# Reordering the second expert's output sums, and the loads and first matmuls, in a linear attention + MoE + top-1 MoE kernel

## The chip, the core and the metric

The kernel runs on one core of a Trainium2 chip. The metric is the device time of one execution in microseconds (us), taken as the median of the runs. The kernel works in f32 with exact splits of operands into a high and a low part.

## What is computed

Three blocks stand one behind the other. Cut to what matters:

```
# attention, B=2, H=8, S=576, D=64, 128 features
phi(x) = exp(h - max(h)) / sqrt(m),   h = x @ omega.T - |x|^2/2
kv = phi(k).T @ v;  z = sum(phi(k));  out = phi(q) @ kv / (phi(q) @ z + 1e-6)
# MoE 1: 1152 tokens, 512 -> 2048 -> 512
x = gelu_sigmoid(x @ w_in) @ w_out
# MoE 2, top-1: 8 experts, 512 -> 1024 -> 512, capacity 288
expert = argmax(x @ w_gate);  out[i] = gate_weight[i] * relu(x[i] @ w1[e]) @ w2[e]
```

## The kernel before, in words

Every product is three matmuls, high x high, high x low and low x high, added up in PSUM (`mm3`, L100 to L103). Tokens go in four groups of 288 (`GS`), which are columns of the tiles; d_model is four chunks of 128 partitions (`KD`), and an expert's inner width of 1024 is eight chunks m (`NF2`).

**The start.** `om_raw` (omega, twice side by side), then the rows of k, v, k, q, v are loaded on SyncE's queue (SP), each batch and half of the heads with one or two DMAs for its first 512 tokens and two small ones, the "tails", for its last 64 (`load_rows`, L110). TensorE (PE) transposes omega (L164); VectorE (DVE) scales it and splits it into `om_hi` and `om_lo` (L188 to L192). A software pipeline of steps s then does, for four rows of k or q at a time, transposition (`do_T`, L295), split (ScalarE, ACT, at L298; DVE at L305), projection (`do_P`), row maximum (L321), exp (L334), and for k the sums `kvp` (L352). Tile's scheduler fixes each engine's order when the kernel is built; every engine then works through its own list in order.

**The end.** MoE 1 and the two experts run as slots n: in each, `do_h2` makes one inner chunk (12 matmuls into `h_ps`, of which there are two buffers), ACT and DVE turn it into the high and low part of its relu (L876, L877), and two slots later `do_y2` adds that chunk's share to all four output chunks, which are held in four PSUM banks:

```
for c in range(KD):
    dc = slice(c * 128, c * 128 + 128)
    mm3(zps[key][c][:, :GS], hi[:, m % 4, dc], lo[:, m % 4, dc], hhi, hlo, m == 0, m == NF2 - 1)
```

Expert 1 (the second, `key` 1) follows expert 0 slot by slot. Its weights come as eight pieces `eraw` of 512 KB into four buffers; `split_e` turns each into a high part (ACT, `eh`, L863) and a low one (DVE, `el`, L864), and a buffer is loaded again after that. When an expert's sums are full, `slot_z` copies the four banks to `z` (DVE L894, ACT L892), and `slot_rows` does, for each of three blocks of 96 tokens, four transposes into one bank (L899), a masked copy of 96x512 into `base` (`copy_predicated`, DVE L940), the gate weight on ACT (L941) and a store on SP (L942). For expert 0 this lies among expert 1's slots; for expert 1 it comes behind the last sum. Then every engine reads three counters and branches past a fallback (L1030 to L1033) that these inputs do not enter.

Of the kernel before, what the change touches and what calls it, by code (L numbers as in the profile page):

```python
# [35 lines left out]
def linear_attention__moe__top1_moe_kernel(  # L36
# [73 lines left out]
    def load_rows(src, kind, b, p, parts=1):  # L110
        t = attA.tile([128, NU, D], F32, tag="raw", name="qk_raw", bufs=6)
        heads = src[b, 4 * p:4 * p + 4]
        per = 4 // parts
        for i in range(parts):
            hs_ = slice(i * per, (i + 1) * per)
            nc.sync.dma_start(
                out=t[:, JF * per * i:JF * per * (i + 1)].rearrange("p (h j) d -> p h (j d)", j=JF),
                in_=heads[hs_, 0:SF].rearrange("h (p j) d -> p h (j d)", j=JF),
            )
        for h in range(2):  # L120
            nc.sync.dma_start(
                out=t[64 * h:64 * h + 64, 16:18],
                in_=heads.rearrange("(u h) s d -> h s u d", h=2)[h, SF:S],
            )
        raws[kind, b, p] = t
# [4 lines left out]

    om_raw = attA.tile([128, 2, D], F32, name="om_raw")
    nc.sync.dma_start(out=om_raw, in_=omega.unsqueeze(1).to_broadcast([M, 2, D]))
    load_rows(k, "k", 0, 0, parts=2)
    load_rows(v, "v", 0, 0)
    load_rows(k, "k", 0, 1)
    load_rows(q, "q", 0, 0)
    load_rows(v, "v", 0, 1)


    ones_bf = const.tile([TT, 128], BF16, name="ones_bf")  # L140
    nc.vector.memset(ones_bf, 1.0)
    col_minus_p = attA.tile([128, 128], I32, name="col_minus_p")
    nc.gpsimd.iota(col_minus_p, pattern=[[1, 128]], base=0, channel_multiplier=-1)
    ident = const.tile([128, 128], F32, name="ident")
# [16 lines left out]
    om_lo = attA.tile([128, 2, M], F32R, name="om_lo")  # L161
    om_f = attA.tile([128, M], F32, name="om_f")
    ps = bank("A", "om_ps")
    nc.tensor.transpose(ps[:, 0:128], om_raw.rearrange("m a d -> m (a d)"), ident)  # L164
    def place_v(b, p, after=None):
        t = raws.pop(("v", b, p))
        eng = nc.gpsimd if b or p else nc.vector
# [20 lines left out]
    nc.vector.tensor_scalar(om_f, ps[:, 0:M], -scale, None, ALU.mult)  # L188
    for h in range(2):
        r = slice(64 * h, 64 * h + 64)  # L190
        nc.vector.tensor_copy(om_hi[r, h], om_f[r])
        nc.vector.tensor_tensor(om_lo[r, h], om_f[r], om_hi[r, h].bitcast(F32), ALU.subtract)  # L192
    om_hi2 = om_hi.rearrange("p a m -> p (a m)")
    om_lo2 = om_lo.rearrange("p a m -> p (a m)")
# [416 lines left out]
    def slot(n, f):  # L611
        side.setdefault(round(n * 2) / 2, []).append(f)
# [3 lines left out]
    def parts_tile(three):  # L616

        nth[0] += 1
        if three and nth[0] % 3 == 0:
            t = gp.tile([128, 2, GS], F32R, tag="wt", name="ghl", bufs=3)  # L620
            return t[:, 0], t[:, 1]
        return [gp.tile([128, GS], F32R, tag=tag, name=tag, bufs=2) for tag in ("ghi", "glo")]
# [242 lines left out]

    hs, zps = {}, {}

    def do_h2(key, m, wt, tok):
        ps = bank("A", "h_ps")
        hi, lo = wt[m // 4]  # L870
        fc = slice((m % 4) * 128, (m % 4) * 128 + 128)
        for c in range(KD):
            mm3(ps[:, :GS], hi[:, c, fc], lo[:, c, fc], x_hi[:, c, :, tok], x_lo[:, c, :, tok],
                c == 0, c == KD - 1)
        hhi, hlo = parts_tile(True)
        nc.scalar.activation(hhi, ps[:, :GS], ACTF.Relu)  # L876
        nc.vector.scalar_tensor_tensor(hlo, ps[:, :GS], 0.0, hhi.bitcast(F32), ALU.max, ALU.subtract)  # L877
        hs[key, m] = (hhi, hlo)

    def do_y2(key, m, wt):  # L880
        if m == 0:
            zps[key] = y_banks()
        hhi, hlo = hs.pop((key, m))
        hi, lo = wt[2 + m // 4]
        for c in range(KD):
            dc = slice(c * 128, c * 128 + 128)
            mm3(zps[key][c][:, :GS], hi[:, m % 4, dc], lo[:, m % 4, dc], hhi, hlo, m == 0, m == NF2 - 1)

    def do_z_out(key, z):
        for c in range(KD):  # L890
# [5 lines left out]
    def z_rows(z, j):  # L896
        ps = mbank("zt_ps")
        for c in range(KD):
            nc.tensor.transpose(ps[:TT, c * 128:(c + 1) * 128], z[:, c, j * TT:(j + 1) * TT], ident)  # L899
        return ps[:TT, :DM]  # L900

    st = {}

# [28 lines left out]
    def slot_base(i):  # L932
        nc.gpsimd.memset(st["s", i][1], 0.0)
# [59 lines left out]
    for i in range(8):  # L993
        if i < 4:
            slot(NSL + 4, lambda i=i: load_e(st["e", 1], i, 1))
        slot(NSL + 5 + i // 2, lambda i=i: split_e(st["w1"], i, 1))
        if i < 4:
            slot(NSL + 5 + i // 2, lambda i=i: load_e(st["e", 1], i + 4, 1))
    slot(NSL + 9, count_left)
    slot(NSL + 9, do_weights)  # L1000
    slot(NSL + NF2 + 1, lambda: slot_z(0))
    slot(NSL + NF2 + 1, lambda: slot_base(0))
    slot(NSL + NF2 + 3, lambda: slot_rows(0, 0))
    slot(NSL + NF2 + 3, lambda: slot_rows(0, 1))
    slot(NSL + NF2 + 4, lambda: slot_rows(0, 2))

    for n in range(NSL + 2 * NF2 + 2):
        now[0] = n
        if n < NSL:
            do_h(*seq[n])  # L1010
        elif n < NSL + 2 * NF2:
            i, m = divmod(n - NSL, NF2)
            do_h2(i, m, st[f"w{i}"], tokens(2 * i))
        for f in side.pop(n - 0.5, []):
            f()
        if 2 <= n < NSL + 2:
            do_consume(*seq[n - 2])
        elif n >= NSL + 2:
            i, m = divmod(n - 2 - NSL, NF2)
            do_y2(i, m, st[f"w{i}"])  # L1020
        for f in side.pop(n, []):
            f()

    slot_z(1)
    slot_base(1)
    for j in range(TJ):
        slot_rows(1, j)


    n_left = nc.values_load(st["all"][0:1, 0:1], min_val=0, max_val=NP)  # L1030
# [91 lines left out]
```

## Time and profile before

| what | before |
| --- | --- |
| median of 3 runs | 332.81 us (332.39 to 333.35) |
| the profiled execution's own time | 333.84 us |
| its span | 331.9 us |
| PE busy | 317.0 us, 96% of the span |
| DVE, ACT, POOL busy | 178.2, 169.7, 52.3 us |
| DMA, mean over the span | 106 GB/s |

The span is what the profile's rows cover; the execution's own time is 1.94 us longer. PE's matmuls are pipelined and their ends are modelled, so a busy PE can still be a PE that waits for a clock.

### The profile page before, as it was taken

The numbers are of one execution on the slowest core, as the hardware profiler recorded it, in microseconds if no ns is written. First come the engines' busy times: TensorE is split into PE (matmuls) and PEld (weight loads), VectorE is DVE, ScalarE is ACT, GpSimd is POOL, SyncE is SP. The second block draws the span as 40 slices with busy tenths as digits, with TensorE's granted clock in tenths as the row PEclk, the third lists the DMA queues.
The fourth block names the chain that finished last, engine by engine and source line by source line (L and its number), as shares of the span: only waits on it lengthen the run. The fifth ranks groups of instructions, "written<-read, shape, count | busy, mean of one in ns | idle before, by whom it ended". The sixth has DMA issues, their size and how long they took to land.

```text
span 331.9 us, 6635 instructions
## 1 busy us (share of the span) xinstructions
PE 317.0 (96%) x2569; PEld 304.0 (92%) x2569; DVE 178.2 (54%) x444; ACT 169.7 (51%) x445; POOL 52.3 (16%) x77
## 2 busy tenths in 40 slices
PE   5899999999999999999999999999999999998990
PEld 4899999899999999999999998989999999998990
DVE  5568888788579764464544223036614134467222
ACT  2788988889744554454544442234614233364312
POOL 3120311130000143434545200000000001100000
PEclk9999999999999999999999999999999999999996
DMA  6999632410032644344431000704400000482202
GB/s 159 289 292 308 209 136 63 129 61 5 2 126 67 225 157 126 128 128 126 146 124 51 0 2 0 254 2 128 126 2 0 3 0 2 161 264 82 73 0 81
DMA packets 29078, 35.18 MB, mean 106 GB/s; under 512 B 5360, under 2 KB 23792, under 8 KB 29040
## 3 DMA queue, kind: packets, MB, share of 16 engines
q1 hardware_dynamic: 29040, 34.69, 33.8%
q8 instruction: 22, 0.36, 0.5%
q14 instruction: 16, 0.13, 0.1%
HBM read 32.33 MB, written 2.36 MB: 105 GB/s over the span
## 4 chain that ended last, share of the span: by engine, by line
PE 87%; DMA 5%; ACT 2%; SPq 2%; DVE 1%; issue 1%; ACTq 0%; DVEq 0%
PE h_ps L101 13%; PE h_ps L102 12%; PE h_ps L103 12%; PE y L101 7%; PE y L102 7%; PE y L103 7%; PE kvp L352 4%; PE nps L377 4%; DMA eraw<-in_moe_w_dram 3%; PE pj L101 2%; PE t L366 2%; PE pj L102 2%; PE pj L103 2%; PE tp L295 2%; PE wt_ps L505 2%; DMA qk_raw<-in_q_dram 2%
## 5 line engine op out<-in xcount | busy, mean ns | idle before, releaser
L640 DVE TENSOR_TENSOR glo<-g,ghi 128x288 fp32r<-128x288 f32 x27 | 12.3, 457 | 39.0 <-ACT g L639 39.0
L633 ACT ACTIVATE g<-h_ps 128x288 f32<-128x288 f32 x32 | 13.2, 411 | 30.0 <-PE h_ps L103 25.1
L321 DVE TENSOR_REDUCE nb<-pj 128x4 f32<-128x512 f32 (+1 forms) x40 | 25.0, 630 | 4.8 <-PE pj L103 4.3
L249 DVE TENSOR_SCALAR wf<-wraw 128x512 int32<-128x512 int32 x32 | 13.4, 423 | 24.9 <-POOL win2l L262 10.8
L864 DVE TENSOR_TENSOR el<-eraw,eh 128x1024 fp32r<-128x1024 f32 x16 | 19.5, 1222 | 13.0 <-ACT eh L863 13.0
L101 PE MATMUL pj<-om_hi,xh 128*128 128x256 f32 x72 | 24.3, 338 | 0.7 <-ACT qp L334 0.6
L637 ACT ACTIVATE ghi<-h_ps 128x288 fp32r<-128x288 f32 x27 | 11.1, 411 | 26.8 <-PE h_ps L103 26.8
L863 ACT CAST eh<-eraw 128x1024 fp32r<-128x1024 f32 x16 | 16.7, 1048 | 14.6 <-PE h_ps L102 7.4
L255 DVE SCALAR_TENSOR_TENSOR wf<-wraw,wf 128x512 int32<-128x512 int32 x32 | 22.9, 716 | 0.4
L334 ACT ACTIVATE qp<-pj,nb 128x128 f32<-128x128 f32 x72 | 21.9, 392 | 0.2
L252 DVE SCALAR_TENSOR_TENSOR wf<-wraw,wf 128x512 int32<-128x512 int32 x32 | 21.8, 685 | 0.2
L102 PE MATMUL pj<-om_lo,xh 128*128 128x256 f32 x72 | 21.4, 298 | 0.0
L334 ACT ACTIVATE kp<-pj,nb 128x128 f32<-128x128 f32 x72 | 21.4, 387 | 0.0
L103 PE MATMUL pj<-om_hi,xl 128*128 128x256 f32 x72 | 21.2, 294 | 0.0
L298 ACT CAST xh<-tp 128x256 fp32r<-128x256 f32 (+1 forms) x40 | 14.6, 364 | 11.5 <-PE tp L295 11.2
L101 PE MATMUL h_ps<-x_hi,win0h 128*128 128x288 f32 x64 | 20.0, 313 | 0.0
L352 PE MATMUL kvp<-vt,kp 128*128 128x65 f32 (+1 forms) x144 | 19.8, 270 | 0.0
L101 PE MATMUL h_ps<-x_hi,win3h 128*128 128x288 f32 x64 | 19.7, 307 | 0.0
L101 PE MATMUL h_ps<-x_hi,win2h 128*128 128x288 f32 x64 | 19.6, 306 | 0.0
L101 PE MATMUL h_ps<-x_hi,win1h 128*128 128x288 f32 x64 | 19.4, 303 | 0.0
L305 DVE TENSOR_TENSOR xl<-tp,xh 128x256 fp32r<-128x256 f32 (+1 forms) x40 | 15.6, 390 | 6.8 <-ACT xh L298 6.6
L101 PE MATMUL h_ps<-x_hi,eh 128*128 128x288 f32 x64 | 19.3, 301 | 0.0
(250 smaller groups left out, 1073.8 us busy)
## 6 DMA issues: line engine op xcount, KB each, us to landing
wraw<-in_moe_w_in_dram SPq DMA_DIRECT2D x16, 512.0 KB, 4.4
wraw<-in_moe_w_out_dram SPq DMA_DIRECT2D x16, 512.0 KB, 3.6
eraw<-in_moe_w_dram SPq DMA_DIRECT2D x16, 512.0 KB, 4.7
qk_raw<-in_v_dram SPq DMA_DIRECT2D x4, 512.0 KB, 5.3
qk_raw<-in_q_dram SPq DMA_DIRECT2D x4, 512.0 KB, 5.7
qk_raw<-in_k_dram SPq DMA_DIRECT2D x3, 512.0 KB, 5.7
out_dram<-zer SPq DMA_DIRECT2D x2, 576.0 KB, 5.5
out_dram<-base SPq DMA_DIRECT2D x6, 192.0 KB, 2.8
```

Of the source, the lines that this page charges most:

```text
L101: nc.tensor.matmul(o, lh, rh, start=start, stop=False)
L102: nc.tensor.matmul(o, lh, rl, start=False, stop=False)
L103: nc.tensor.matmul(o, ll, rh, start=False, stop=stop)
L252: nc.vector.scalar_tensor_tensor(f, high, -0x40000000, f, ALU.bitwise_and, ALU.bitwise_or)
L255: nc.vector.scalar_tensor_tensor(f, low, 29, f, ALU.logical_shift_right, ALU.bitwise_or)
L298: nc.scalar.copy(xh[:, :n], tp[:, :n])
L305: nc.vector.tensor_tensor(xl[:, :n], tp[:, :n], xh[:, :n].bitcast(F32), ALU.subtract)
L321: mark["M", s] = nc.vector.tensor_reduce(nb[:, :nj], pj[:, :nj * M].rearrange("p (a m) -> p a m", m=M), AX, ALU.min)
L334: nc.scalar.activation(t[:, i], pj[:, i * M:(i + 1) * M], ACTF.Exp, bias=nb[:, i:i + 1], scale=-1.0)
L352: nc.tensor.matmul(ps[:, o:o + n], kp[:, i], vts[p][:, u, c0:c0 + n], start=(f == 0), stop=(f == NU - 1))
L863: nc.scalar.copy(hi, tv)
L864: nc.vector.tensor_tensor(lo, tv, hi.bitcast(F32), ALU.subtract)
```

## The change

It does five things. (1) The tails of the first k go out from ACT's queue instead of SP's, behind a one-column copy on ACT. (2) Seven small bf16 matmuls into an unused bank stand ahead of omega's transposition on PE, four behind it; their results are not read. (3) One of the two casts to `om_hi` goes from DVE to ACT. (4) Expert 1's chunks m = 1 to 7 are kept in tiles of their own, its `do_h2` run without `do_y2` between them, and the last four pieces of its weights are split one to two slots apart, each behind the last relu. (5) `do_last` makes the output sums with the output chunk c outside: m = 0 to 3, then the chunk before goes out (three transposes, masked copy of 96x3x128, gate weight, one store), then m = 4 to 7. Expert 0's rows are worked on within chunk 0. Only chunk 3 is left behind the last sum, in three pieces of 96 tokens with banks and tiles of their own.

```diff
--- before.py
+++ after.py
@@ -118,7 +118,7 @@
                 in_=heads[hs_, 0:SF].rearrange("h (p j) d -> p h (j d)", j=JF),
             )
         for h in range(2):
-            nc.sync.dma_start(
+            (nc.scalar if parts > 1 else nc.sync).dma_start(
                 out=t[64 * h:64 * h + 64, 16:18],
                 in_=heads.rearrange("(u h) s d -> h s u d", h=2)[h, SF:S],
             )
@@ -130,15 +130,25 @@
 
     om_raw = attA.tile([128, 2, D], F32, name="om_raw")
     nc.sync.dma_start(out=om_raw, in_=omega.unsqueeze(1).to_broadcast([M, 2, D]))
-    load_rows(k, "k", 0, 0, parts=2)
+    ones_bf = const.tile([TT, 128], BF16, name="ones_bf")
+    nc.vector.memset(ones_bf, 1.0)
+    first = attA.tile([TT, 1], F32, name="first")
+    with tc.issue_after(nc.scalar.copy(first, ones_bf[:, 0:1]).ins):
+        load_rows(k, "k", 0, 0, parts=2)
     load_rows(v, "v", 0, 0)
     load_rows(k, "k", 0, 1)
     load_rows(q, "q", 0, 0)
     load_rows(v, "v", 0, 1)
 
 
-    ones_bf = const.tile([TT, 128], BF16, name="ones_bf")
-    nc.vector.memset(ones_bf, 1.0)
+    idle = bank("M", "idle")
+
+    def spin(n):
+        for _ in range(n):
+            nc.tensor.matmul(idle[:, 0:256], ones_bf, ones_bf.unsqueeze(1).to_broadcast([TT, 2, 128]),
+                             start=True, stop=True)
+
+    spin(7)
@@ -161,7 +171,8 @@
     om_lo = attA.tile([128, 2, M], F32R, name="om_lo")
     om_f = attA.tile([128, M], F32, name="om_f")
     ps = bank("A", "om_ps")
-    nc.tensor.transpose(ps[:, 0:128], om_raw.rearrange("m a d -> m (a d)"), ident)
+    with tc.issue_after(nc.tensor.transpose(ps[:, 0:128], om_raw.rearrange("m a d -> m (a d)"), ident).ins):
+        spin(4)
@@ -188,7 +199,7 @@
     nc.vector.tensor_scalar(om_f, ps[:, 0:M], -scale, None, ALU.mult)
     for h in range(2):
         r = slice(64 * h, 64 * h + 64)
-        nc.vector.tensor_copy(om_hi[r, h], om_f[r])
+        (nc.scalar.copy if h else nc.vector.tensor_copy)(om_hi[r, h], om_f[r])
         nc.vector.tensor_tensor(om_lo[r, h], om_f[r], om_hi[r, h].bitcast(F32), ALU.subtract)
     om_hi2 = om_hi.rearrange("p a m -> p (a m)")
@@ -865,6 +876,8 @@
 
     hs, zps = {}, {}
 
+    spare = {}
+
     def do_h2(key, m, wt, tok):
         ps = bank("A", "h_ps")
         hi, lo = wt[m // 4]
@@ -872,9 +885,15 @@
         for c in range(KD):
             mm3(ps[:, :GS], hi[:, c, fc], lo[:, c, fc], x_hi[:, c, :, tok], x_lo[:, c, :, tok],
                 c == 0, c == KD - 1)
-        hhi, hlo = parts_tile(True)
-        nc.scalar.activation(hhi, ps[:, :GS], ACTF.Relu)
-        nc.vector.scalar_tensor_tensor(hlo, ps[:, :GS], 0.0, hhi.bitcast(F32), ALU.max, ALU.subtract)
+        if key == 1 and m:
+            for s in "hl":
+                if s not in spare:
+                    spare[s] = pool_of["in", 2].tile([128, NF2 - 1, GS], F32R, tag=f"win2{s}", name=f"hh{s}")
+            hhi, hlo = spare["h"][:, m - 1], spare["l"][:, m - 1]
+        else:
+            hhi, hlo = parts_tile(True)
+        mark["ra"] = nc.scalar.activation(hhi, ps[:, :GS], ACTF.Relu)
+        mark["rv"] = nc.vector.scalar_tensor_tensor(hlo, ps[:, :GS], 0.0, hhi.bitcast(F32), ALU.max, ALU.subtract)
         hs[key, m] = (hhi, hlo)
 
     def do_y2(key, m, wt):
@@ -886,6 +905,13 @@
             dc = slice(c * 128, c * 128 + 128)
             mm3(zps[key][c][:, :GS], hi[:, m % 4, dc], lo[:, m % 4, dc], hhi, hlo, m == 0, m == NF2 - 1)
 
+    def split_late(i):
+        if i < 4:
+            split_e(st["w1"], i, 1)
+        else:
+            with tc.issue_after(mark["ra"].ins), tc.issue_after(mark["rv"].ins):
+                split_e(st["w1"], i, 1)
+
     def do_z_out(key, z):
         for c in range(KD):
             if c % 2:
@@ -898,6 +924,63 @@
         for c in range(KD):
             nc.tensor.transpose(ps[:TT, c * 128:(c + 1) * 128], z[:, c, j * TT:(j + 1) * TT], ident)
         return ps[:TT, :DM]
+
+    def do_last(wt):
+
+        z, base = scratch(1)
+        nc.gpsimd.memset(base, 0.0)
+        zps[1] = y_banks()
+        mk = st["mk", 1].bitcast(I32)
+        r0 = 2 * GS
+        g0 = 2 * TJ
+        rows = out[r0:r0 + GS, :].rearrange("(j p) d -> p j d", p=TT)
+
+        def sums(c, ms):
+            dc = slice(c * 128, c * 128 + 128)
+            for m in ms:
+                hhi, hlo = hs[1, m]
+                hi, lo = wt[2 + m // 4]
+                mm3(zps[1][c][:, :GS], hi[:, m % 4, dc], lo[:, m % 4, dc], hhi, hlo, m == 0, m == NF2 - 1)
+
+        def chunk(c):
+            dc = slice(c * 128, c * 128 + 128)
+            ps = mbank("zt_ps")
+            for j in range(TJ):
+                nc.tensor.transpose(ps[:TT, j * 128:(j + 1) * 128], z[:, c, j * TT:(j + 1) * TT], ident)
+            nc.vector.copy_predicated(base[:, :, dc], mk.unsqueeze(2).to_broadcast([TT, TJ, 128]),
+                                      ps[:TT, :TJ * 128].rearrange("p (j d) -> p j d", j=TJ))
+            nc.vector.tensor_tensor(base[:, :, dc], base[:, :, dc],
+                                    gw[:, g0:g0 + TJ].unsqueeze(2).to_broadcast([TT, TJ, 128]), ALU.mult)
+            nc.sync.dma_start(out=rows[:, :, dc], in_=base[:, :, dc])
+
+        half = NF2 // 2
+        for c in range(KD):
+            sums(c, range(half))
+            if c:
+                chunk(c - 1)
+            else:
+                slot_rows(0, 0)
+                slot_rows(0, 1)
+            sums(c, range(half, NF2))
+            if c == 0:
+                slot_rows(0, 2)
+            if c < KD - 1:
+                nc.scalar.copy(rows_of(z[:, c]), in_order(zps[1][c][:, :GS]))
+        c = KD - 1
+        dc = slice(c * 128, c * 128 + 128)
+        pss = [mbank("zt_ps"), mbank("zt_ps"), bank("A", "zt_ps")]
+        zl = [z[:, c, 0:TT]] + [pool_of["out", 0].tile([128, 2048], F32, tag=f"wout0{s}", name="zl")[:, 0:TT] for s in "hl"]
+        for j in range(TJ):
+            nc.vector.tensor_copy(rows_of(zl[j]), in_order(zps[1][c][:, :GS])[:, j * TT // JF:(j + 1) * TT // JF])
+        for j, ps in enumerate(pss):
+            nc.tensor.transpose(ps[:TT, 0:128], zl[j], ident)
+            nc.vector.copy_predicated(base[:, j, dc], mk[:, j:j + 1].to_broadcast([TT, 128]), ps[:TT, 0:128])
+            if j < TJ - 1:
+                nc.scalar.activation(base[:, j, dc], base[:, j, dc], ACTF.Copy, scale=gw[:, g0 + j:g0 + j + 1])
+            else:
+                nc.vector.tensor_scalar(base[:, j, dc], base[:, j, dc], gw[:, g0 + j:g0 + j + 1], None, ALU.mult)
+        nc.sync.dma_start(out=rows[:, 0, dc], in_=base[:, 0, dc])
+        nc.sync.dma_start(out=rows[:, 1:, dc], in_=base[:, 1:, dc])
 
     st = {}
 
@@ -993,16 +1076,13 @@
     for i in range(8):
         if i < 4:
             slot(NSL + 4, lambda i=i: load_e(st["e", 1], i, 1))
-        slot(NSL + 5 + i // 2, lambda i=i: split_e(st["w1"], i, 1))
+        slot(NSL + (5, 5, 6, 6, 9, 11, 12, 14)[i], lambda i=i: split_late(i))
         if i < 4:
             slot(NSL + 5 + i // 2, lambda i=i: load_e(st["e", 1], i + 4, 1))
     slot(NSL + 9, count_left)
     slot(NSL + 9, do_weights)
     slot(NSL + NF2 + 1, lambda: slot_z(0))
     slot(NSL + NF2 + 1, lambda: slot_base(0))
-    slot(NSL + NF2 + 3, lambda: slot_rows(0, 0))
-    slot(NSL + NF2 + 3, lambda: slot_rows(0, 1))
-    slot(NSL + NF2 + 4, lambda: slot_rows(0, 2))
 
     for n in range(NSL + 2 * NF2 + 2):
         now[0] = n
@@ -1017,14 +1097,12 @@
             do_consume(*seq[n - 2])
         elif n >= NSL + 2:
             i, m = divmod(n - 2 - NSL, NF2)
-            do_y2(i, m, st[f"w{i}"])
+            if i == 0:
+                do_y2(i, m, st[f"w{i}"])
+            elif m == NF2 - 1:
+                do_last(st[f"w{i}"])
         for f in side.pop(n, []):
             f()
-
-    slot_z(1)
-    slot_base(1)
-    for j in range(TJ):
-        slot_rows(1, j)
 
 
     n_left = nc.values_load(st["all"][0:1, 0:1], min_val=0, max_val=NP)
```

**Where instructions stand now: the start, SP and ACT.** `qk_raw` are the loaded rows, the 64x2x64 ones the tails. SP's list before:

```order
L132 DMA om_raw<-in_omega_dram 128x2x64
L116 DMA qk_raw<-in_k_dram 128x2x256 x2
L121 DMA qk_raw<-in_k_dram 64x2x64 x2
L116 DMA qk_raw<-in_v_dram 128x4x256
L121 DMA qk_raw<-in_v_dram 64x2x64 x2
```

SP's list now:

```order
L132 DMA om_raw<-in_omega_dram 128x2x64
L116 DMA qk_raw<-in_k_dram 128x2x256 x2
L116 DMA qk_raw<-in_v_dram 128x4x256
L121 DMA qk_raw<-in_v_dram 64x2x64 x2
L116 DMA qk_raw<-in_k_dram 128x4x256
```

ACT's list now (before it had the table load and then the casts to `xh`):

```order
L136 ACT_TABLE_LOAD
L136 CAST first<-ones_bf 96x1
L121 DMA qk_raw<-in_k_dram 64x2x64 x2
L202 CAST om_hi<-om_f 64x128
L309 CAST xh<-tp 128x256 x4
```

The order of omega and k on SP is as it was; two issues have left SP's list ahead of v, and stand on ACT ahead of its first cast.

**Expert 1's weights and relus on ACT.** `eh` are pieces of weights, `ghi`, `ghl` and `hhh` relus, `z` expert 0's sums. Before:

```order
L863 CAST eh<-eraw 128x1024
L876 ACTIVATE ghl<-h_ps 128x288
L863 CAST eh<-eraw 128x1024
L892 COPY z<-y_3733 128x288
L892 COPY z<-y_3735 128x288
L863 CAST eh<-eraw 128x1024
L876 ACTIVATE ghi<-h_ps 128x288
L863 CAST eh<-eraw 128x1024
```

Now:

```order
L895 ACTIVATE hhh<-h_ps 128x288
L874 CAST eh<-eraw 128x1024
L918 COPY z<-y_3747 128x288
L918 COPY z<-y_3749 128x288
L895 ACTIVATE hhh<-h_ps 128x288 x2
L874 CAST eh<-eraw 128x1024
L895 ACTIVATE hhh<-h_ps 128x288
L874 CAST eh<-eraw 128x1024
L895 ACTIVATE hhh<-h_ps 128x288 x2
L874 CAST eh<-eraw 128x1024
```

The copies of `z` now stand behind one late piece instead of two, and the last three pieces stand between the relus of a stretch in which PE does nothing but `do_h2`.

**The end on DVE.** Before:

```order
L894 COPY z<-y_4100 128x288
L894 COPY z<-y_4102 128x288
L940 COPY_PREDICATED base<-p_mk,zt_ps 96x512 x3
L1030 TENSOR_LOAD all_ni
```

Now:

```order
L950 COPY_PREDICATED base<-p_mk,zt_ps 96x3x128
L952 TENSOR_TENSOR base<-base,gw 96x3x128
L974 COPY z<-y_4194 128x96
L974 COPY zl<-y_4194 128x96 x2
L977 COPY_PREDICATED base<-p_mk,zt_ps 96x128 x3
L981 TENSOR_SCALAR base<-base,gw 96x128
L1108 TENSOR_LOAD all_ni
```

Behind the last sum DVE has seven short instructions where it had a copy of 128x288 and three masked copies of 96x512.

## Rows read from the trace of the kernel before

**Rows 1.** the page, part 4, whole span: the chain that ended last, by engine

```profile
PE 87%; DMA 5%; ACT 2%; SPq 2%; DVE 1%; issue 1%; ACTq 0%; DVEq 0%
```

**Rows 2.** the chain, 0 to 20 us: start us, us, what it was

```profile
2.29 0.73 SPq L121
...
3.70 0.60 SPq L116
...
7.57 5.96 DMA qk_raw<-in_q_dram
...
13.67 0.30 PE tp L295
```

**Rows 3.** waits of PE, whole span: us in total, times, longest

```profile
PE tp L295 <- DMA qk_raw<-in_q_dram: 1.3, 1, 1.3
...
PE y L101 <- ACT z L892: 0.9, 1, 0.9
...
PE y L101 <- DVE z L894: 0.4, 1, 0.4
```

**Rows 4.** windows: us, busy us of each engine, PEclk, DMA share, GB/s

```profile
2.30:4.20 1.90, 0.44 (x1) 0.18 (x1) 0.97 (x5) 0.00 (x0) 1.59 (x9) 1.00 0.92 254
4.20:5.60 1.40, 1.11 (x4) 0.71 (x4) 0.71 (x3) 0.37 (x1) 0.00 (x0) 1.00 0.69 111
...
9.00:13.50 4.50, 3.38 (x25) 3.04 (x24) 3.44 (x9) 3.04 (x12) 0.00 (x0) 1.00 1.00 296
13.70:40.00 26.30, 26.30 (x238) 26.30 (x238) 18.45 (x48) 22.57 (x79) 5.92 (x10) 1.00 0.95 286
```

**Rows 5.** timeline of PE, 9 to 10.1 us: start us, us, engine line op

```profile
9.00 0.41 PE L103 MATMUL pj<-om_hi,xl 128*128 128x256 f32 x1
...
10.04 0.28 PE L103 MATMUL pj<-om_hi,xl 128*128 128x256 f32 x1
```

**Rows 6.** timeline of ACT, 293 to 303 us: idle before and releaser in brackets

```profile
293.81 1.05 ACT L863 CAST eh<-eraw 128x1024 fp32r<-128x1024 f32 x1 [2.78 <-DMA eraw<-in_moe_w_dram]
...
302.25 1.05 ACT L863 CAST eh<-eraw 128x1024 fp32r<-128x1024 f32 x1 [1.00 <-DMA eraw<-in_moe_w_dram]
```

**Rows 7.** groups of ACT by form: count | busy us, mean ns

```profile
L863 ACT CAST eh<-eraw 128x1024 fp32r<-128x1024 f32 x16 | 16.7, 1048 | 14.6 <-PE h_ps L102 7.4 <-DMA eraw<-in_moe_w_dram 6.3 <-PE y L102 0.8
...
L876 ACT ACTIVATE ghi<-h_ps 128x288 fp32r<-128x288 f32 x10 | 4.1, 410 | 10.5 <-PE h_ps L103 10.4
```

**Rows 8.** groups of DVE by form: count | busy us, mean ns

```profile
L864 DVE TENSOR_TENSOR el<-eraw,eh 128x1024 fp32r<-128x1024 f32 x16 | 19.5, 1222 | 13.0 <-ACT eh L863 13.0
L305 DVE TENSOR_TENSOR xl<-tp,xh 128x256 fp32r<-128x256 f32 x32 | 13.4, 419 | 6.8 <-ACT xh L298 6.6
...
L877 DVE SCALAR_TENSOR_TENSOR glo<-h_ps,ghi 128x288 fp32r<-128x288 f32 x10 | 4.5, 453 | 8.1 <-ACT ghi L876 8.0
...
L305 DVE TENSOR_TENSOR xl<-tp,xh 128x128 fp32r<-128x128 f32 x8 | 2.2, 275 | 0.0
```

**Rows 9.** timeline, 322 us to the end

```profile
322.38 0.30 PE L103 MATMUL y<-ghl,el 128*128 128x288 f32 x1
...
323.60 2.18 DVE L940 COPY_PREDICATED base<-p_mk,zt_ps 96x512 f32<-96x512 int32 x3 [0.82 <-PE zt_ps L899]
324.35 2.18 ACT L941 ACTIVATE base<-base,gw 96x512 f32<-96x512 f32 x3 [1.23 <-DVE base L940]
...
324.37 0.64 PE L899 MATMUL zt_ps<-ident,z 128*96 128x128 f32 x4 [0.66 <-DVE base L940]
325.10 1.77 SPq L942 DMA_DIRECT2D out_dram<-base  x3
```

**Rows 10.** instructions of L1033, 300 us to the end: duration ns, first and last start

```profile
L1033 SPq EVENT_SEMAPHORE  x9: 17/17/17, 329.8 to 330.4; - x9
...
L1033 PEldq COMPARE_BRANCH  x1: 4094/4094/4094, 325.8 to 325.8; - x1
```

**Rows 11.** instructions of L942, 300 us to the end: issue to landing

```profile
DMA to landing us min/median/max: 2.1/2.8/4.1
```

## The prediction

> **What bounds the kernel now.** I read the chain that ended last first. It runs through PE for 87% of the span [rows 1], so time is won only where the chain leaves PE, or where PE has less to do. It leaves PE at the start, for a moment when expert 1 begins its output sums, and at the end.
>
> *Start.* The chain there is SP's queue, one issue behind the other: the two k tails from 2.29 us, v at 3.70, q at 7.57; then q's transfer of 5.96 us; then PE's first transposition of q at 13.67 [rows 2]. PE waited 1.3 us for it [rows 3]. While the tails were issued little came in: 111 GB/s at a DMA share of 0.69 between 4.2 and 5.6 us, against 296 GB/s at 1.00 between 9 and 13.5 [rows 4]. From 13.7 to 40 us PE is busy 26.30 of 26.30 us [rows 4], so what it gains before 13.7 it keeps.
>
> *Middle.* At 299 to 301 us PE waits 0.9 and 0.4 us for expert 0's sums to leave their banks [rows 3], because those copies stand behind weight splits on ACT and DVE. Nothing else holds PE for long after that.
>
> *End.* The last sum ends at 322.68, which I call T (322.38 + 0.30). Behind it stand transposes, three masked copies of 0.73 us, three scalings of 0.73 and three stores; the last store is issued at 325.10 + 1.77 - 0.32 = 326.55, taking an issue as 0.32 us (estimate from a store's start to the group's end) [rows 9]. The span closes at 331.9, T + 9.2.
>
> **The change part by part.** I sum against the profiled execution (333.84 us, span 331.9), which stood 0.3% above the median of 332.81, and apply the difference to the median.
>
> *K tails on ACT.* Two issues leave SP ahead of v: 3.70 - 2.29 = 1.41 us [rows 2]. Everything on SP up to q is issued that much earlier. The tails still move their bytes, now beside v; ACT issues them in a stretch in which it does no work (0.00 us busy from 2.3 to 4.2 us [rows 4]), and the cast of `om_hi` that stands behind them replaces 0.3 us of DVE, so both cost nothing while k's rows are still on their way. The gain is at most 1.41 and, if the 16 DMA engines were the limit and not the issue, nothing. The rows speak for the issue up to 9 us: at 0.69 the engines had room. After 9 us they are full [rows 4], which eats some of it, as do the tails themselves. I take **-1.2**, between 0 and -1.4.
>
> The Trainium skill, "Trainium Kernel Development and Optimization", Key Constraints, says that DMAs issued from several engines run on the same 16 DMA engines and that a second issuer saves only the sequencer's issue time. By that rule the term lies between 0 and the issue time too; where the engines are the limit it is 0, which is the first rival.
>
> *Small matmuls.* PE works at the lower of its two levels until about 9.2 us: the same 256 columns take 0.41 us at 9.00 and 0.28 at 10.04 [rows 5]. The difference of 0.13 is near the 0.11 between 256 columns at 1.2 and at 2.4 GHz; the PEclk column shows 1.00 all the while, so I go by durations. Eleven matmuls of 256 columns are about 11 x 0.21 = 2.3 us at the lower level, in a PE that did one matmul between 2.3 and 4.2 us [rows 4]; they cover nothing up, and cost nothing unless omega's transposition comes behind them. If the level rises earlier, PE reaches q's rows sooner, but q's rows set when it goes on. They are worth at most the 0.1 us by which PE's wait (1.3) is shorter than the 1.41 above, and a margin. **0.0**, between -0.1 and +0.5 (some of the first seven ahead of omega).
>
> *The order of the attention.* With the loads, Tile's order of the attention steps moves slightly: the third step of decoding the first weights comes earlier on DVE and its cast earlier on ACT. In 13.7 to 40 us DVE has 18.45 of 26.30 us busy and ACT 22.57 [rows 4], so both have room: **0.0**, +-0.3. POOL's list does not change.
>
> *Expert 1's sums late.* The wait for the banks goes, 0.9 + 0.4 us [rows 3]: expert 1's sums now begin six `do_h2` later. **-1.3**. What is late next: PE runs `do_h2` alone, 12 matmuls of some 0.13 us, 1.6 us for each chunk, on two buffers. Each chunk needs 0.41 us of ACT and 0.45 of DVE, and a late split takes 1.05 on ACT and 1.22 on DVE [rows 7, 8]: with a split 1.46 and 1.67 us. Over one chunk DVE is 0.07 late, over two with a split each 0.14, and the split that still stands ahead of a relu costs its part of the slack. I take **+0.3**, between 0 and +0.6.
>
> *Chunks leaving one by one.* PE's sums are the same 96 matmuls. Of the 12 transposes behind the last sum, 9 move ahead of it: 9 x 0.12 = **+1.1** on PE before the end, 0.12 being (0.64 - 0.28) / 3, the spacing of four transposes [rows 9]. Masked copies, gate weights and stores of chunks 0 to 2 lie beside 3.2 us of sums each: a masked copy of 384 columns is under the 0.73 of 512 [rows 9], its scaling on DVE no dearer, 1.5 of 3.2 us. Expert 0's rows go the same way, on ACT. SP has five stores instead of three; only the last two count.
>
> *Behind the last sum.* DVE's forms of 256 and 128 columns are 0.42 and 0.28 us [rows 8], so 96 columns come to 0.24 and a small form of 128 to 0.28. Three copies of 96 columns end at T + 0.04 + 0.72 = T + 0.76, three masked copies at T + 1.6, the last scaling at T + 1.9, and the last store is issued at T + 1.95, against T + 3.9 now. ACT's two scalings and the first store lie beside this. So the last issue comes 1.95 us earlier. What follows is less sure. SP's nine semaphore steps run from 329.8 to 330.4, and PE's branch past the fallback takes 4.09 us from 325.8, to 329.9 [rows 10]: two things end together, and stores take 2.1 to 4.1 us to land [rows 11]. Lower bound: PE's branch keeps its length; it follows the last transposition, at about T + 0.8, by three register loads, so it begins near T + 2.3 instead of T + 3.1, and the gain is 0.8. Upper bound: only landing counts, and a half as large store lands in 2.1 instead of the third one's 3.7 (330.3 - 326.55): 1.95 + 1.6 = 3.5. I take **-1.5**, nearer to the branch, whose row is the plainer one.
>
> Sum: -1.2 + 0.0 + 0.0 - 1.3 + 0.3 + 1.1 - 1.5 = **-2.6 us**: 331.2 for the profiled execution, **330.2 us** for the median, 0.8% faster.
>
> **The rivals.**
>
> *DMA engines, not issue, hold q.* For it: share 1.00 from 9 us on, and a transfer that takes 5.96 us after its issue [rows 2, 4]. Against it: the 0.69 before. It takes away 1.2: 331.4 us.
>
> *Landing alone ends the kernel.* For it: the times to land spread to 4.1 with three stores close together [rows 11], and smaller ones leave earlier now. Against it: PE's branch ends no earlier than SP's steps begin. It gives 2.0 more: 328.2 us.
>
> *Little moves.* The first rival together with the lower bound of the end and the upper one of the buffers: -1.3 + 0.6 + 1.1 - 0.8 = -0.4, 332.4 us.
>
> *Late splits hold up expert 1* (slower). If a piece of weights lands after ACT has come to its cast, ACT stands there with the relus behind it, both buffers fill, and PE stops where it had output sums to do before. That happened to ACT already: 2.78 us at 293.81, 1.00 at 302.25 [rows 6]. A split that stands whole between a chunk and its relu costs 1.05 + 0.41 + 0.45 + 1.22 = 3.1 us [rows 7, 8] where two buffers give 1.6; three such lose 4.5: 330.2 - 0.3 + 4.5 = 334.4 us. It decides from the point where a late piece lands after about 305 us; the last one landed at 302.25, 3 us before, and the loads start as early as before.
>
> That the small matmuls do not raise the clock at all would change at most 0.1 us here and is no case of its own.
>
> **How the numbers follow.** The forecast has 0.55, with 329.2 to 331.2 as its own range from the bounds of its terms; DMA-bound start 0.17; landing alone 0.10; little moves 0.12; late splits 0.06. A change of 0.3%, 1.0 us, is about what a measurement can tell from none. The first three are faster by more: 0.82. Little moves is the same: 0.12. Late splits are slower: 0.06. The range 328.3 to 331.9 takes in the forecast, the DMA-bound start and the nearer half of the landing case; left out are late splits, little moves and the far end of landing, some 2 in 10.
>
> **What would show it.** Start: q issued on SP near 6.2 us, PE's first transposition of q near 12.4 instead of 13.67, and 256 columns at 0.28 us well before 9. If q is issued at 6.2 and still lands at 13.5, the first rival is right. Middle: no wait of PE for `z`, and waits of at most 0.6 us in all for buffers of `h_ps` between 297 and 307 us; longer ones behind a cast that waits for a DMA would be the slower rival. End: last sum to the end of the span 7.7 us instead of 9.2; PE's branch still 4 us, if I have weighed it rightly. Waits of PE between 14 and 100 us that are not there now would mean that the reordered attention cost something I put at nothing.

## The result, and the profile after

| what | before | after |
| --- | --- | --- |
| median | 332.43 us (6 runs, 331.94 to 333.35) | 329.74 us (6 runs, 329.09 to 330.20) |
| ratio | | 0.9903, 95% interval 0.9875 to 0.9931 |
| profiled execution, its span | 333.84, 331.9 us | 330.05, 328.0 us |

The ratio is an estimate of its own and not the quotient of the two medians, which is 0.992. The change makes the kernel faster by 2.7 us on the medians. The prediction was 330.2 us, -2.6. The two profiled executions are 3.9 us apart in span, 1.2 more than the medians, since the one of before lay above every other run of its kernel. So a difference between these two traces is not yet one between the kernels.

The page of the changed kernel, parts 1 and 4:

```profile
PE 318.8 (97%) x2580; PEld 305.8 (93%) x2580; DVE 180.8 (55%) x451; ACT 168.7 (51%) x447; POOL 52.7 (16%) x77
...
PE 95%; ACT 1%; DMA 1%; DVE 0%; issue 0%; SPq 0%; ACTq 0%
```

PE has 95% of the chain where it had 87 [rows 1], and DMA 1% where it had 5: q's transfer is no longer a link. Its waits, whole span (us in total, times, longest):

```profile
PE idle L148 <- DVE ones_bf L134: 1.1, 1, 1.1
PE pj L101 <- ACT qp L345: 0.4, 1, 0.4
PE zt_ps L976 <- DVE z L974: 0.4, 1, 0.4
PE tp L306 <- DMA qk_raw<-in_k_dram: 0.3, 1, 0.3
```

The waits for q (1.3) and for expert 0's banks (0.9 and 0.4) [rows 3] are gone, and none for `h_ps` has come.

**Start.** ACT's queue issues the tails while SP issues k. SP's queue (start us, us):

```profile
2.29 0.47 SPq L116 DMA_DIRECT2D qk_raw<-in_v_dram  x1
...
6.15 0.59 SPq L116 DMA_DIRECT2D qk_raw<-in_q_dram  x1
```

q is issued at 6.15 instead of 7.57 [rows 2], and takes 5.0 us to about 11.15. The windows beside [rows 4]:

```profile
4.20:5.60 1.40, 1.20 (x5) 0.80 (x5) 0.59 (x3) 0.46 (x2) 0.00 (x0) 1.00 0.99 274
9.00:13.50 4.50, 4.50 (x35) 4.30 (x34) 3.35 (x9) 3.09 (x12) 0.28 (x1) 1.00 0.87 255
```

The engines that stood at 0.69 and 111 GB/s from 4.2 to 5.6 us now move 274. From 9 to 13.5 us PE is busy throughout, for 3.38 of 4.50 us before. What holds PE now is its own level (timeline of PE):

```profile
10.17 0.38 PE L102 MATMUL pj<-om_lo,xh 128*128 128x256 f32 x1
10.38 0.28 PE L103 MATMUL pj<-om_hi,xl 128*128 128x256 f32 x1
...
12.28 0.27 PE L306 MATMUL tp<-ident,qk_raw 128*128 128x128 f32 x1
```

256 columns take 0.28 us from 10.38 on; before they did from 9.57 on, with eleven matmuls fewer ahead. PE reaches q's rows at 12.28 instead of 13.67, 1.1 us after they landed. ACT's exps stand close behind as the next bound: in `e8_oldsplit` (below), whose lists are the same up to there, the rise comes at 9.4, the first `kvp` then wait for the exps one after the other, and PE comes to q's rows at 12.30 all the same.

**End.** Timeline behind the last sum, which ends at 319.81 + 0.29 = 320.10:

```profile
319.81 0.29 PE L103 MATMUL y<-hhh,el 128*128 128x288 f32 x1
...
320.14 0.26 DVE L974 COPY z<-y 128x96 f32<-128x96 f32 x1 [0.41 <-PE y L103]
320.31 0.41 DVE L974 COPY zl<-y 128x96 f32<-128x96 f32 x2
...
320.81 0.71 DVE L977 COPY_PREDICATED base<-p_mk,zt_ps 96x128 f32<-96x128 int32 x3
...
321.56 0.28 DVE L981 TENSOR_SCALAR base<-base,gw 96x128 f32<-96x128 f32 x1
321.62 0.33 SPq L982 DMA_DIRECT2D out_dram<-base  x1
322.05 0.37 SPq L983 DMA_DIRECT2D out_dram<-base  x1
```

The last store is issued at T + 1.95, as worked out, and the span ends at T + 7.9 (before T + 9.2). The instructions of the fallback's branch, L1111 (duration ns, first and last start us):

```profile
L1111 SPq EVENT_SEMAPHORE  x9: 17/17/17, 325.9 to 326.5; - x9
...
L1111 PEldq COMPARE_BRANCH  x1: 3397/3397/3397, 322.2 to 322.2; - x1
L1111 SPq COMPARE_BRANCH  x1: 45/45/45, 322.5 to 322.5; - x1
...
L1111 DVEq COMPARE_BRANCH  x1: 72/72/72, 323.4 to 323.4; - x1
...
L1111 DVEq EVENT_SEMAPHORE  x1: 21/21/21, 326.6 to 326.6; - x1
```

PE's branch takes 3.4 us (4.1 before, [rows 10]). But SP, too, does nothing between its branch at 322.5 and 325.9, and DVE nothing between 323.4 and 326.6. DVE is the last to come past it; I had read PE's row alone. In the kernel before it was ACT:

```profile
L1033 ACTq COMPARE_BRANCH  x1: 50/50/50, 328.0 to 328.0; - x1
...
L1033 ACTq EVENT_SEMAPHORE  x1: 17/17/17, 330.6 to 330.6; - x1
```

Being last past the branch is not yet being what ends the kernel. SP's closing steps show no wait in the changed kernel:

```profile
L1195 SPq EVENT_SEMAPHORE  x12: 17/28/28, 326.5 to 327.9; - x12
```

### The profile page after: what moved, and what is told of

Its sections match the earlier page's. It is cut to its first block, busy times and chain, and to the rows that moved or that the text cites. A ratio compares the mean times of both kernels' runs of the same rounds, so it can differ in the third digit from the quotient of the medians.

```text
span 328.0 us, 6667 instructions
## 1 busy us (share of the span) xinstructions
PE 318.8 (97%) x2580; PEld 305.8 (93%) x2580; DVE 180.8 (55%) x451; ACT 168.7 (51%) x447; POOL 52.7 (16%) x77
## 4 chain that ended last, share of the span: by engine, by line
PE 95%; ACT 1%; DMA 1%; DVE 0%; issue 0%; SPq 0%; ACTq 0%
PE h_ps L101 14%; PE h_ps L102 13%; PE h_ps L103 13%; PE y L101 8%; PE y L102 8%; PE y L103 8%; PE kvp L363 5%; PE nps L388 4%; PE pj L101 3%; PE tp L306 3%; PE pj L102 3%; PE pj L103 3%; PE t L377 3%; PE wt_ps L516 2%; PE lgt_ps L696 1%; PE wg_ps L526 1%
## 5 line engine op out<-in xcount | busy, mean ns | idle before, releaser
L260 DVE TENSOR_SCALAR wf<-wraw 128x512 int32<-128x512 int32 x32 | 13.4, 423 | 24.7 <-POOL win2l L273 10.7
L266 DVE SCALAR_TENSOR_TENSOR wf<-wraw,wf 128x512 int32<-128x512 int32 x32 | 22.9, 717 | 0.4
L263 DVE SCALAR_TENSOR_TENSOR wf<-wraw,wf 128x512 int32<-128x512 int32 x32 | 22.5, 708 | 0.2
L103 PE MATMUL h_ps<-x_hi,win0l 128*128 128x288 f32 x64 | 19.2, 300 | 0.0
L102 PE MATMUL h_ps<-x_lo,win0h 128*128 128x288 f32 x64 | 19.2, 300 | 0.0
```

Source lines behind the costliest of these rows:

```text
L102: nc.tensor.matmul(o, lh, rl, start=False, stop=False)
L103: nc.tensor.matmul(o, ll, rh, start=False, stop=stop)
L260: nc.vector.tensor_scalar(f, high, 3, 0x3FFFFFF8, ALU.logical_shift_left, ALU.bitwise_and)
L263: nc.vector.scalar_tensor_tensor(f, high, -0x40000000, f, ALU.bitwise_and, ALU.bitwise_or)
L266: nc.vector.scalar_tensor_tensor(f, low, 29, f, ALU.logical_shift_right, ALU.bitwise_or)
```

## The experiments

Theory at the outset: the start gives about half, by q's earlier issue and by something in the attention's order; the end gives the other half; the small matmuls do nothing by the clock. Each kernel was timed in five rounds beside the kernel before, which took 332.4, 332.3 and 331.9 us in the three groups (e1 to e4; e5 to e8; e9 to e12). The changed kernel was timed beside 332.43 us only, in the runs of the result. So where a kernel of the third group is set against its 329.74, the two kernels before are 0.5 us apart, and so much of a difference need not be the kernels'.

### The start alone

`e1_start`: the kernel before with the diff's parts (1) to (3).

> The kernel before with the change's start alone (k tails on ScalarE, the eleven small matmuls, one cast of om_hi on ScalarE); the end is the old one. Theory: the start is worth what the last transposition of the attention showed between the two traces, 1.4 us at q and about 2.0 us by 78 us: 330.4 to 331.0 us where the kernel before takes 332.4, PE's first transposition of q at 12.3 +-0.3 instead of 13.67. Rival: part of the 2.0 us was only that one execution of the kernel before was a slow one (333.84 against a median of 332.4); then the start is worth 0.5 to 1.0: 331.4 to 331.9. Waits of PE for z (0.9 + 0.4 us) are back in both.

330.93 us, ratio 0.996 (0.9945 to 0.9975): -1.4 us, at the upper end of the theory's range. q's first transposition is at 12.21, and the attention's last one is won by 2.05 us against the profiled execution of before (77.65 for 79.70). The medians give 1.4, so part of the 2.05 was that execution, as the rival says; `e2_end`, which has the old start, does its last transposition at 79.11, 1.46 behind this one. PE's waits at the end:

```profile
PE zt_ps L910 <- DVE base L951: 0.7, 1, 0.7
PE y L101 <- DVE z L905: 0.5, 2, 0.4
```

The wait for the banks is 0.5 us in the old end with the new start, not 1.3.

### The end alone

`e2_end`: the changed kernel with the old start.

> The changed kernel with the old start (tails on SP, no small matmuls, both casts on VectorE); the end is the new one. Theory: waits for z -1.3, nine transpositions +1.0, behind the last sum -1.3, nothing for buffers: -1.6, so 330.8 us; q first transposed near 13.7. Rival one: the rest of the end does nothing but pay for the transpositions, 331.8 or more. Rival two: the end carries nearly all of the 2.7 us, 329.9 or less, and the start little. Start and end act on stretches that PE keeps apart, so the two parts should add up to 2.7 +-0.4.

331.00 us, ratio 0.9969 (0.9954 to 0.9984): -1.4 us. With e1 it adds up to -2.8, for -2.7 in the change. PE waits 1.1 us for q again and not at all for banks. Behind the last sum (321.07 + 0.29) stand 7.6 us.

### Without the small matmuls

`e3_nospin`:

```diff
-    spin(7)
-    with tc.issue_after(nc.tensor.transpose(ps[:, 0:128], ...).ins):
-        spin(4)
+    nc.tensor.transpose(ps[:, 0:128], ...)
```

> The changed kernel without the eleven small matmuls. Theory: they do nothing; 256 columns of f32 take 0.41 us until 9 to 10.4 us either way, so 329.7 +-0.4 us, the same as the changed kernel. Rival one: they raise the clock in most executions and the profiled one was an exception: 330.3 to 331.0. Rival two: they put the rise off (10.2 us with them against 9.2 in the kernel before): without them the rise is at 9.2 and the time 329.1 or less.

330.13 us, ratio 0.9939 (0.9921 to 0.9956): 0.4 above the changed kernel, at the edge of the theory's range. The clock is not the reason: here 256 columns take 0.28 us from 8.8 us on, earlier than in the changed kernel. The time is lost later. First `nps` and last `tp` (timeline of PE), in the kernel before:

```profile
26.54 0.72 PE L377 MATMUL nps<-kvs,qt 128*128 128x65 f32 x5
...
79.70 0.27 PE L295 MATMUL tp<-ident,qk_raw 128*128 128x128 f32 x1
```

in the changed kernel:

```profile
25.43 1.06 PE L388 MATMUL nps<-kvs,qt 128*128 128x65 f32 x8
...
77.72 0.27 PE L306 MATMUL tp<-ident,qk_raw 128*128 128x128 f32 x1
```

and without the small matmuls:

```profile
25.08 1.06 PE L379 MATMUL nps<-kvs,qt 128*128 128x65 f32 x8
...
78.31 0.27 PE L297 MATMUL tp<-ident,qk_raw 128*128 128x128 f32 x1
```

53.2, 52.3 and 53.2 us. The lists of PE, ACT and DVE differ between them in this stretch: with the matmuls that nobody reads, Tile's scheduler writes the attention in another order. Why it does was not looked into.

### The tails back on SP

`e4_tails_sp`: `nc.scalar if parts > 1 else nc.sync` is `nc.sync` again.

> The changed kernel with the k tails back on SP; small matmuls and the cast on ScalarE stay. Theory: SP's queue held q, so q is issued 1.4 us later, at 7.6 us, and PE waits for it again: first transposition of q at 13.4 to 13.7, 1.2 to 1.4 us slower: 330.9 to 331.1. Rival: PE at its lower level is the bound up to q now, and landing 1.4 us later than 11.15 us costs only 0.3 us there: 330.0.

331.77 us, ratio 0.9983 (0.9971 to 0.9995): 2.0 above the changed kernel, more than either. PE's waits:

```profile
PE tp L306 <- DMA qk_raw<-in_q_dram: 0.8, 1, 0.8
...
PE t L377 <- ACT wt L518: 0.3, 1, 0.3
...
PE xps L430 <- DVE xr L408: 0.3, 1, 0.3
```

q's first transposition is at 13.00, 0.7 us behind the changed kernel. The rest arises later, in the attention, whose lists differ again on PE, ACT and DVE: first `nps` and last `tp` are here

```profile
25.89 1.06 PE L388 MATMUL nps<-kvs,qt 128*128 128x65 f32 x8
...
79.83 0.27 PE L306 MATMUL tp<-ident,qk_raw 128*128 128x128 f32 x1
```

53.9 us apart, 1.65 more than in the changed kernel; the waits for `wt` and `xr`, which the changed kernel does not have, are 0.6 of it. By the end of the last sum this kernel is 2.1 us behind, 322.22 for 320.10. So "undo one edit" undid two things, and this run does not price the tails by themselves.

### Four, seven

`e5_four` takes the seven out, `e6_seven` the four. Without the seven, each engine's list but for them is word for word that of the changed kernel; without the four, it is that of the kernel without any, but for the seven.

> The changed kernel with the four small matmuls behind omega's transposition but without the seven ahead of it; every engine's list is else as in the changed kernel, word for word. Theory: what the small matmuls do is done by the four, by the order in which the scheduler then writes the attention (52.3 us from the first nps to the last tp, against 53.2 without them), not by PE's clock: 329.7 +-0.3 us, the same as the changed kernel; 256 columns still take 0.41 us until some moment between 8 and 10.2 us. Rival: the seven warm PE up; without them 330.2 or more.

329.59 us, ratio 0.9921 (0.9907 to 0.9936), 52.3 us from first `nps` to last `tp`; 256 columns at 0.41 us until 10.1. The theory holds.

> The changed kernel with the seven small matmuls ahead of omega's transposition but without the four behind it; the attention stands in the order of the kernel without any of them. Theory: order is what counts, so 53.2 us from the first nps to the last tp and 330.2 +-0.3 us, as without any. Rival: the seven count by the clock; then 329.7 with 52.3 us or with a rise of the clock before 8 us.

330.65 us, ratio 0.9955 (0.9938 to 0.9972), 0.15 above the theory's range, and 53.2 us:

```profile
25.36 1.06 PE L388 MATMUL nps<-kvs,qt 128*128 128x65 f32 x8
...
78.59 0.27 PE L306 MATMUL tp<-ident,qk_raw 128*128 128x128 f32 x1
```

So the seven are worth nothing that shows, and the four about 0.9 us in this stretch, by the order: the lists differ by nothing else there, and PE is at full pace all through it. The medians give the four 1.1 us (e6 less e5) or 0.4 (e3 less the changed kernel); e3 and e6 have one order and overlap in their intervals.

### No gap on PE

`e7_fill` puts `spin(6)` for `spin(4)`, and `spin(2)` behind the first four transpositions of k.

> The changed kernel with two more small matmuls behind omega's transposition and two between the first four transpositions of k and the first projection, where PE stood 0.3 us each, so that PE works without a gap from 1.1 us on; the attention's order stays. Theory: these matmuls do not lift PE's level earlier, and delay k by up to 0.2 us: 329.7 to 330.0, 256 columns at 0.41 us until 8 to 10.2 us. Rival: it was the two gaps that kept the level down; without them it rises before 7 us, some 15 matmuls take 0.1 us less each, PE reaches q at about 11, and the time is 328.3 to 329.0.

329.12 us (328.56 to 330.80), ratio 0.9923 (0.9903 to 0.9944): between the theory's range and the rival's. In the profiled execution, the fastest of the six, PE's pace rises at 7.0 us, as the rival has it (timeline of PE):

```profile
6.93 0.37 PE L101 MATMUL pj<-om_hi,xh 128*128 128x256 f32 x1
7.14 0.28 PE L102 MATMUL pj<-om_lo,xh 128*128 128x256 f32 x1
...
11.32 0.30 PE L306 MATMUL tp<-ident,qk_raw 128*128 128x128 f32 x1 [0.26 <-DMA qk_raw<-in_q_dram]
```

There q's rows become the bound again, at 11.3 us. (The edit also moves a few matmuls and a cast of the first steps among each other; from first `nps` to last `tp` it is 52.2 us.) One profile is one execution, so two more kernels, with `spin(8)` ahead of omega and with none:

> The kernel with the gaps filled (6 small matmuls behind omega, 2 behind the first transpositions of k), with an eighth small matmul ahead of omega as well. Theory one: a PE without gaps from 1.1 us on is lifted to its higher level at 7 to 8 us instead of 8.1 to 10.2; PE then waits 0.2 to 0.5 us for q's rows and the time is 328.6 to 329.3. Theory two: the rise at 7.0 us in the one profile was chance, as the spread from 8.1 to 10.2 in the others; then the rise here is again between 8 and 10.2 and the time 329.4 to 329.9.

329.42 us, ratio 0.9918 (0.9899 to 0.9938), and the rise comes late, as theory two has it, though PE has no gap of 0.1 us from 1.1 us on:

```profile
9.73 0.53 PE L101 MATMUL pj<-om_hi,xh 128*128 128x256 f32 x1
10.09 0.29 PE L102 MATMUL pj<-om_lo,xh 128*128 128x256 f32 x1
```

> The same filled gaps behind omega (6 and 2), without any small matmul ahead of it: PE works without a gap from about 3 us on instead of from 1.1. If the work from 1.1 us on is what lifts the level early, the rise comes at 8 us or later and the time is 329.4 to 329.9. If closing the two gaps is enough, the rise is at 7 to 8 us and the time 328.6 to 329.3, and the seven are worth nothing here either.

329.11 us, ratio 0.9915 (0.9894 to 0.9937), rise at 7.5:

```profile
7.50 0.38 PE L103 MATMUL pj<-om_hi,xl 128*128 128x256 f32 x1
...
8.18 0.28 PE L103 MATMUL pj<-om_hi,xl 128*128 128x256 f32 x1
```

With the gaps filled the rise came at 7.0, 7.5 and 9.9 us; in the kernels without filled gaps it lay between 8.0 (e2) and past 10.7 (e9, where the matmul at 10.38 still takes 0.41), with small matmuls or without. An early rise carries through to the end: the last sum ends at 318.76 in e7 and 319.10 in e12, against 320.08 in e11 and 320.10 in the changed kernel. But that filling the gaps brings an early rise is not shown, since e11 fills them too. The three medians are 0.2 to 0.6 below 329.74 and 329.59, inside the intervals, and against the kernel before of their own groups they are -3.2, -2.5 and -2.8 us, where the changed kernel has -2.7. Whether filling helps stays open.

### Late splits at the old places

`e8_oldsplit`: `(5, 5, 6, 6, 9, 11, 12, 14)[i]` is `5 + i // 2` again, and the late ones no longer stand behind a relu.

> The changed kernel with the last four pieces of expert 1's weights split where the kernel before splits them, ahead of the relus of m = 2 to 7 instead of between them. Theory: the last pieces land near 297 and 300 us, ScalarE stands at their casts with the relus behind, both buffers of h_ps fill and PE stops for 2 to 3 us: 331.5 to 333. Rival: the pieces land early enough and the new slots are worth nothing: 329.7 +-0.3.

331.29 us (330.36 to 332.65), ratio 0.9975 (0.996 to 0.9991): 1.6 above the changed kernel, below the theory's 2 to 3 and far from the rival's 0. ACT's timeline, 292 to 299 us:

```profile
292.85 1.05 ACT L874 CAST eh<-eraw 128x1024 fp32r<-128x1024 f32 x1 [0.29 <-DMA eraw<-in_moe_w_dram]
...
295.33 1.05 ACT L874 CAST eh<-eraw 128x1024 fp32r<-128x1024 f32 x1 [1.11 <-DMA eraw<-in_moe_w_dram]
...
298.12 1.05 ACT L874 CAST eh<-eraw 128x1024 fp32r<-128x1024 f32 x1
```

and what it does to PE:

```profile
299.60 0.40 PE L101 MATMUL h_ps<-x_hi,eh 128*128 128x288 f32 x1 [0.94 <-DVE hhl L896]
```

This is the mechanism of my slower rival at a third of its price of 4.5: ACT waits 1.4 us for pieces, relus stand behind, the buffers fill and PE stops once. That stop and what else this trace shows account for 1.0 of the 1.6 (its span is 329.0 for 328.0); the rest is seen in the medians alone.

### The last store, and the fallback

`e9_nolast` leaves out `nc.sync.dma_start(out=rows[:, 1:, dc], ...)`; `e10_nobranch` leaves out all from `n_left = ...` on.

> The changed kernel without its very last store: rows 96 to 287 of the last group of 128 output columns are not written. The store before it is issued 0.4 us earlier and landed 1.5 us after its issue, at 323.1, where the last one landed at about 325.4. Theory: PE's way past the fallback (its branch ended at 325.6) ends the kernel together with the last landing, so taking the landing away alone gives at most 0.3 us: 329.4 to 329.7. Rival: landing alone ends it; then the end comes up to 2.2 us earlier: 327.4 to 328.5.

329.46 us, ratio 0.9922 (0.9902 to 0.9942): no landing to wait for, and at most 0.3 us won. DVE's step behind the branch is still the last, at 326.7 of 327.7 us. SP comes past the branch 0.9 us earlier than in the changed kernel (325.0 for 325.9), and now one of its closing steps waits 0.6 us:

```profile
L1194 SPq EVENT_SEMAPHORE  x12: 17/28/602, 325.6 to 327.7; - x12
```

By these rows DVE ends the kernel here, where SP ended the changed kernel's profile. From the last sum to the end it is 7.5 us for 7.9; that need not be the store, since e3 and e11 have 7.5 with both stores.

> The changed kernel without the fallback for pairs that are left over, and so without the three counters that every engine reads and the branch of 3.4 us on PE; the output is that of these inputs. The two stores at the end stay. Theory: the branch and the landing end nearly together, so taking the branch away alone gives 0.2 to 0.6 us: 329.1 to 329.5, and the engines' last semaphore steps stand right behind the last landing. Rival: the branch was the later of the two by much and landing was waiting on it in some way; then 2 to 3.5 us: 326.2 to 327.7.

327.00 us, ratio 0.9847 (0.9825 to 0.9869): 2.7 us below the changed kernel, the rival's range. Against the kernels before of their own groups it is 2.3 (4.9 less 2.7), and between the two traces, from the last sum on, 3.0. The last store is issued 1.9 us behind the last sum as in the changed kernel, and the span closes at 325.1, 4.9 us behind the sum's end at 320.25 instead of 7.9. The row of the store in the page's list of DMA issues (KB, us to landing), changed kernel and this one:

```profile
out_dram<-base SPq DMA_DIRECT2D x1, 96.0 KB, 3.3
```

```profile
out_dram<-base SPq DMA_DIRECT2D x1, 96.0 KB, 1.8
```

Without the branch the store lands at 324.0. So branch and landing do not end together: the way past the fallback ends the kernel, 2.3 to 3.0 us behind what the stores need. Why the same store takes 3.3 us to land with the fallback no run tells. The edit takes out the counters' loads together with the branch, so the price is that of both.

What the engines stand for behind the branch is not shown, but the list of DMA queues names a candidate. Packets of the kind "instruction" on queue 14, whole span, changed kernel and this one:

```profile
q14 instruction: 16, 0.13, 0.1%
```

```profile
q14 instruction: 10, 0.08, 0.1%
```

In the changed kernel four packets of this kind (queues 8 and 14) move between 323 and 325 us, while the engines stand, and none between 288 and 290, where POOL comes past; here none moves from 318 us to the end of the span. That the engines wait for these packets is argued from the times only.

This is not a version to use, since other inputs need the fallback. A faster kernel of the same function is not settled by these runs.

## Why the prediction was right

The sum and its two halves held: start -1.2 predicted and -1.4 measured (e1), end -1.3 + 0.3 + 1.1 - 1.5 = -1.4 predicted and -1.4 measured (e2). Inside the start two errors made up for each other: that the sum of the start came out so close is luck in part.

- *K tails, -1.2.* The mechanism was right: q is issued at 6.15 ("near 6.2") and PE reaches it at 12.28 ("near 12.4"); it is not the first rival's DMA engines that hold it, since PE waits for no transfer there. The size was not 1.2: in the run of the tails alone it is 0.7 at q (13.00 to 12.28), between e2 and e1 0.85 (13.06 to 12.21). What I had not put next in line is PE itself at its lower level: q's rows lay there for 1.1 us.
- *Small matmuls, 0.0.* Right of the clock as far as e3, e5 and e6 show (no difference without the seven), but "256 columns at 0.28 us well before 9" did not come. Wrong of the four: they are worth 0.9 us through the order.
- *The order of the attention, 0.0 +-0.3.* This is the step that failed. Before, 53.2 us lie between first `nps` and last `tp` (79.70 - 26.54); now 52.3 (77.72 - 25.43). Ahead of that, from q's first transposition on, the new order loses 0.3 (13.15 for 12.87), so it wins 0.6 in all, twice my bound (e2 and e1, with the old and the new start, give the same: 53.15 to 52.30 us). I argued from room on DVE and ACT. The lines moved PE's own matmuls among each other, and PE's busy time is modelled: it hid most of the difference: 18.90 of 19 us before and 19.00 now from 33 to 52 us. Which of the moved instructions wins the time no run tells.
- *The banks, -1.3.* Gone, as predicted. How much that is worth depends on the execution: 1.3 in the profile of before, 0.5 in e1. From the attention's last transposition to the end of the last sum it is 242.98 us before and 242.38 now, but 242.24 in e1, which has the old end; so against e1 the banks, the buffers and the transposes together win nothing (the sum has +0.1 for them), and what the end wins it wins behind the last sum.
- *Buffers of `h_ps`, +0.3.* 0.0. DVE's 0.07 us per chunk never added up, as the splits stand one to two chunks apart; e8 shows what they cost when they don't: 0.9 us in one wait.
- *Nine transposes, +1.1.* Three of them cost PE 0.33 us (318.48 - 317.89 less two spacings of 0.13), so nine 1.0.
- *Behind the last sum, -1.5.* 9.2 (in e1 as well) to 7.9 here and 7.5 to 7.6 in e2 to e4. The size was right. The reason was half right: it is the branch and not the landing (e9), which is where the rival "landing alone" falls; but my "two things end together", branch and landing, was not so (e10), and PE is not the engine that comes past the branch last. PE's branch, which I had kept at 4.1 us, took 3.4 here and 3.3 to 4.0 in the runs. What won the time is that SP, DVE and ACT all reach the branch earlier behind the last sum T: SP at T + 2.4 for T + 4.2, DVE at T + 3.3 for T + 4.5, ACT at T + 2.6 for T + 5.3. They come past it 1.2 to 2.0 us earlier (SP 5.8 for 7.1, DVE 6.5 for 7.7, ACT 5.9 for 7.9). DVE gets there because its last instruction ends 1.7 us behind the sum (321.84 - 320.10) where it took 3.1 (325.78 - 322.68, [rows 9]).
- *Late splits, slower, 0.06.* The place was right and the new slots are what prevents it. They are not a detail of the change: with the old slots over half of its gain goes.

## What to carry to other kernels

Where a scheduler writes the order, an edit at the head can move work on every engine for a long way behind it: compare a stretch that the edit does not touch, from one landmark to another, before a gain is booked to the edit. When a wait for a transfer is removed, work out when the waiting engine could have come at all, at the pace that its rows show just there. At the end of a kernel, look for what each engine does between its last instruction and the closing steps, not for the last store alone, and test it by taking one away at a time.

## What the runs showed that I had not expected

- From a branch over code that is not entered to the next instruction it takes 3.2 to 3.4 us on each of PE, SP, ACT and DVE at the end of the changed kernel, and branch and counters together cost 2.3 to 3.0 us of the whole (e10); POOL, which comes to it at 288.7 us, is past it 0.3 us later (289.0). Why POOL is, no run here tells. The Trainium skill, "Advanced Engine Details and Errata", Control Flow Timing, gives some 108 ns for a compare-and-branch; DVE's row of 72 ns is of that size, and what comes behind it is not in it; PE's row of 3397 ns is not.
- PE's pace rose anywhere between 7.0 us and past 10.7 from profile to profile, with the granted-clock column at 1.00 all the while; eleven small bf16 matmuls did not bring it forward. Five profiles (the changed kernel, e1, e8, e9, e10) have the same lists on every engine up to 90 us, and still it rose at 10.3, 10.0, 9.4, past 10.7 and 9.4. What sets the moment stays open. The Trainium skill, "TensorE: Matmul & The Clock Gate", What's actually happening, says that the count of matmuls at the lower level varies from run to run of one kernel and is not to be fitted; these rows agree.
- Four matmuls that nobody reads altered the attention's time by 0.9 us through the scheduler (52.3 us in e5, 53.2 in e6), about as much as q's earlier issue.
